# One ACT function for the second layer's activation, and weight absolute values on DVE

## The chip, the core and the metric

The kernel runs on one core of a Trainium2 chip. The core's engines each work through a queue of their own, in order: TensorE (PE in the profile, with its weight loads as PEld), VectorE (DVE), ScalarE (ACT), GpSimd (POOL) and SyncE (SP, which here only issues transfers). Engines wait for one another through semaphores. The metric is the device time of one execution in microseconds (us), as the median of several runs.

## What is computed

The reference does causal attention with a local mask for half of the heads and a strided mask for the other half (4 sequences of 576 positions, 8 heads of 64), then two feed-forward layers on the 2304 tokens of 512 features, each with 2048 hidden features. Everything is float32. The layers differ in their activation:

```
h = x @ w_in                       # first layer
g = h * clip(h + 3, 0, 6) / 6      # "hard swish"
x = g @ w_out

h = x @ w_in                       # second layer
sp = log1p(exp(h))                 # h itself above 20
g = h * tanh(sp)                   # "Mish"
out = g @ w_out
```

## The kernel before

**Precision.** Each float32 product is made of three matmuls: every operand is split into a high part and a low part (`xh` and `xl` for the layer's input, `gh` and `gl` for the activation's result, `w(0)` and `w(1)` for a weight), and `mm3` adds low weight times high value, high weight times low value and high times high into one PSUM bank (L804, L805, L806).

**Steps.** The tokens are cut into blocks of 512, 512, 512, 256 and 512 columns, and the 16 chunks of 128 hidden features of a layer into groups (4, 6, 6 in the first layer, 6, 5, 5 in the second). One step is one block with one chunk: 80 steps a layer. A step has twelve matmuls that make `h` in a PSUM bank, the activation, the split of the result, and twelve matmuls that add the chunk's share to four banks of output sums. The first kind reads `xh` and `xl`, the second `gh` and `gl`, so they can be told apart in the trace.

**Between the two kinds of matmul.** In the first layer ACT makes a clipped line of `h` from PSUM into a buffer `t` (L812) and DVE multiplies it by `h` (L815). In the second layer `mish` (L820 to L853) does eight passes: Tanh from PSUM (L836), Square (L837), Exp (L839) on ACT, a line that may go to ACT, DVE or POOL (L832, L834), then a DVE product (L843), Square on ACT (L845), a DVE product (L848) and a DVE product with `h` (L852), after which the bank of `h` is free. In both layers the high part is then copied, by ACT in this kernel (`gh`, L337), and the low part subtracted on POOL (`gl`, L900).

**Weights.** They come as 64-bit numbers, in 64 pieces (the input half and the output half of 16 chunks in 2 layers, numbered k from 0 to 63), by one DMA each. `decode` (L738 to L798) takes each apart: absolute value (L759 on ACT or L761 on DVE), then DVE passes (L766, L770, L775), a copy of the high part on ACT (L337), and further DVE passes up to the low part (L781, L785, L789, L793). There are 16 slots for ready weights. A slot is free when the last block of its group has used it.

**Order.** Nothing is ordered by the compiler. `Plan` holds each operation with a cost, the operations it depends on, a bank or two and a due time, and `run` makes a list schedule of it ahead of time: it takes the operation that can start first by these costs, and among those near to each other the one due first. Due times of matmuls follow the steps, those of the activation follow from them backwards. Where an operation may run on several engines, `run` chooses. The instructions are then written out in that order, and every engine keeps to it. A change of a cost or of the number of operations can so move any instruction behind it.

Of the kernel before, what the change touches and what calls it, by code (L numbers as in the profile page):

```python
# [7 lines left out]
F32 = mybir.dt.float32  # L8
# [3 lines left out]
AF = mybir.ActivationFunctionType  # L12
ALU = mybir.AluOpType
PSUM = bass.MemoryType.PSUM

P = 128
# [24 lines left out]
EARLY_SUMS = 2  # L41

N_RAW, N_WA, N_WM, N_T, N_G = 3, 3, 2, 4, 4
N_SEED = 2
N_QKV, N_E, N_PT = 2, 4, 2

BANKS = {
    "first": (0, 1, 2, 3, 4, 5, 6, 7),
# [37 lines left out]

LEAD = 0.8883

SEED = (0.67959831, 1.31360091, 0.35009874)
STEP = (0.1250005420051549, -1.500006504050999, 0.7499978319855396)  # L90


class Op:
# [26 lines left out]
class Plan:  # L120
# [9 lines left out]
    def add(self, engine, cost, emit, deps=(), due=None, bank=None, frees=None, lock=""):  # L130
        costs = cost if isinstance(cost, dict) else {engine: cost}
        op = Op(costs, emit, deps, due, bank, frees, lock)
        self.ops.append(op)
        return op
# [140 lines left out]
def act_ns(n, psum=False):  # L275
    return (50 if psum else 95) + 0.84 * n


def dve_ns(n):
    return 70 + 1.05 * n  # L280
# [6 lines left out]
def copy_ns(n, psum=False):  # L287

    return {"act": act_ns(n, psum), "dve": dve_ns(n if psum else n / 2)}
# [4 lines left out]
    return {"dve": dve_ns(n), "pool": pool_ns(n)}  # L294


def line_ns(n):

    return {"act": act_ns(n), "dve": dve_ns(n / 2), "pool": 50 + 1.05 * n}


def mm3_ns(n):

    return 3 * (n + 32) / 2.4
# [7 lines left out]
def attention_then_two_ffns(ctx, tc, qkv, masks, wts, out):  # L312
# [3 lines left out]
    nc = tc.nc  # L316
    B, NPAIR = qkv.shape[:2]
    DM, NT = out.shape
# [7 lines left out]
    N = max(BLOCKS)  # L326
# [5 lines left out]
    add = plan.add  # L332
    engines = {"dve": nc.vector, "pool": nc.gpsimd}
# [8 lines left out]
    pool = ctx.enter_context(tc.tile_pool(name="main", bufs=1, side="right"))  # L342
# [8 lines left out]
    gh_t = [pool.tile([P, N], F32R, name=f"gh{k}") for k in range(N_G)]  # L351
    gl_t = [pool.tile([P, N], F32R, name=f"gl{k}") for k in range(N_G)]

    offset = pool.tile([P, 1], F32, name="offset")
    raw_t = [pool.tile([P, DM], U64, name=f"raw{k}") for k in range(N_RAW)]
    wa_t = [pool.tile([P, DM], F32, name=f"wa{k}") for k in range(N_WA)]
    wm_t = [pool.tile([P, DM], F32, name=f"wm{k}") for k in range(N_WM)]
# [24 lines left out]
    pt_t = [ap_.tile([P, (HS + 2) * P], F32, name=f"pt{k}") for k in range(N_PT)]  # L382
    zeros = words[:, n_v:][:, :FILL]
    scratch = ap_.tile([P, 1], F32, name="scratch")
    late = []

    def open_late():

        att.__exit__(None, None, None)
        lp = ctx.enter_context(tc.tile_pool(name="late", bufs=1, side="left"))  # L390
        w_t.extend(lp.tile([P, 2, DM], F32R, name=f"w{k}") for k in range(2 * EARLY_SLOTS, 2 * SLOTS))
        ys.extend(lp.tile([P, KC, BLOCKS[j]], F32, name=f"y{j}") for j in range(EARLY_SUMS, len(BLOCKS)))
        late.extend(lp.tile([P, N], F32, name=f"seed{k}") for k in range(N_SEED))


    class Record:
# [3 lines left out]
    for m in range(2):  # L400
        for g, n in enumerate(GROUPS[m]):
            walk = LAST_WALK if (m, g) == (1, len(GROUPS[1]) - 1) else range(len(blocks))
            for j in walk:
                for c in range(n):
                    s = Record()
# [7 lines left out]
    t = START  # L413
# [310 lines left out]
    closing = add("act", 0, open_late, attended)  # L724
# [8 lines left out]
    t = 1e12  # L733
    for k in order[::-1]:
        t = w_due[k] = min(w_due[k] - EARLY_W, t - HALF_PACE)
    w_ready, w_ops = {}, []

    def decode(k):  # L738


        m, c, half = order[k]
        raw, a, rest = raw_t[k % N_RAW], wa_t[k % N_WA], wm_t[k % N_WM]
        words = raw.bitcast(U32).rearrange("p (n t) -> p n t", t=2)
        low, high = words[:, :, 0], words[:, :, 1]
        ai, resti = a.bitcast(U32), rest.bitcast(U32)
        slot = k % (2 * SLOTS)
        w = lambda part: w_t[slot][:, part]
        old = w_ops[k - N_RAW]["raw"] if k >= N_RAW else []
        old_a = w_ops[k - N_WA]["end"] if k >= N_WA else None
        old_m = w_ops[k - N_WM]["end"] if k >= N_WM else None  # L750
        if k >= 2 * SLOTS:
            old_w = w_use[order[k - 2 * SLOTS]]
        else:
            old_w = [closing] if slot >= 2 * EARLY_SLOTS else []
        load = add("dma", dma_ns(8 * P * DM), lambda: nc.sync.dma_start(raw, wts[m, c, half]), old)

        def magnitude(eng):
            if eng == "act":
                nc.scalar.activation(a, high.bitcast(F32), AF.Abs)  # L759
            else:  # L760
                nc.vector.tensor_scalar(ai, high, 0x7FFFFFFF, None, ALU.bitwise_and)  # L761

        o = add(None, copy_ns(DM), magnitude, [load, old_a], lock=("dve",))
        o = add(
            "dve", dve_ns(DM / 2),
            lambda: nc.vector.tensor_scalar(a, a, TINY, HUGE, ALU.max, ALU.min), [o], lock=("dve",),  # L766
        )
        o = add(
            "dve", dve_ns(DM / 2),
            lambda: nc.vector.tensor_scalar(ai, ai, 3, 0x3FFFF000, ALU.logical_shift_left, ALU.bitwise_and),  # L770
            [o], lock=("dve",),
        )
        hi = add(
            "dve", dve_ns(DM),
            lambda: nc.vector.scalar_tensor_tensor(ai, high, 0xC0000000, ai, ALU.bitwise_and, ALU.bitwise_or),  # L775
            [o], lock=("dve",),
        )
        o = add(None, copy_ns(DM), lambda eng: copy(eng, w(0), a), [hi, *old_w], lock=("dve",))
        power = add(
            "dve", dve_ns(DM / 2),  # L780
            lambda: nc.vector.tensor_scalar(ai, ai, 0xFF800000, None, ALU.bitwise_and), [o], lock=("dve",),  # L781
        )
        o = add(
            "dve", dve_ns(DM / 2),
            lambda: nc.vector.tensor_scalar(resti, high, 0x1FF, None, ALU.bitwise_and), [load, old_m], lock=("dve",),  # L785
        )
        o = add(
            "dve", dve_ns(DM),
            lambda: nc.vector.scalar_tensor_tensor(rest, resti, 2.0 ** 32, low, ALU.mult, ALU.add), [o], lock=("dve",),  # L789
        )  # L790
        lo = add(
            "dve", dve_ns(DM),
            lambda: nc.vector.scalar_tensor_tensor(w(1), rest, 2.0 ** -52, a, ALU.mult, ALU.mult),  # L793
            [o, power, *old_w], lock=("dve",),
        )
        lo.due = w_due[order[k]]
        w_ops.append({"raw": [hi, o], "end": lo})
        w_ready[order[k]] = lo  # L798
# [16 lines left out]
            lambda: nc.vector.scalar_tensor_tensor(t, t, 1.0, h(), ALU.min, ALU.mult), [o], frees=s.h,  # L815
        )

    mish_ends = {}

    def mish(s, prod, free):  # L820


        n = s.n
        t = t_t[s.id % N_T][:, :n]
        h = lambda: banks[s.h.n][:, :n]
        seed = lambda: late[s.id % N_SEED][:, :n]
        a, b, c = SEED
        scale, bias, more = STEP

        def line(eng):  # L830
            if eng == "act":
                nc.scalar.activation(seed(), seed(), AF.Copy, bias=a, scale=b)  # L832
            else:
                engines[eng].tensor_scalar(seed(), seed(), b, a, ALU.mult, ALU.add)  # L834

        o = add("act", act_ns(n, True), lambda: nc.scalar.activation(t, h(), AF.Tanh, scale=0.5), [prod, free])  # L836
        o = add("act", act_ns(n), lambda: nc.scalar.activation(t, t, AF.Square, bias=1.0, scale=-1.0), [o])  # L837
        w = o
        o = add("act", act_ns(n), lambda: nc.scalar.activation(seed(), t, AF.Exp, scale=-c), [o, mish_ends.get(s.id - N_SEED), closing])  # L839
        o = add(None, line_ns(n), line, [o], lock=("dve", "pool"))  # L840
        o = add(
            "dve", dve_ns(n),
            lambda: nc.vector.scalar_tensor_tensor(t, t, 4.0, seed(), ALU.add, ALU.mult), [o], lock=("dve",),  # L843
        )
        o = add("act", act_ns(n), lambda: nc.scalar.activation(t, t, AF.Square, bias=offset, scale=scale), [o])  # L845
        o = mish_ends[s.id] = add(
            "dve", dve_ns(n),
            lambda: nc.vector.scalar_tensor_tensor(t, t, more, seed(), ALU.add, ALU.mult), [o], lock=("dve",),  # L848
        )
        return add(  # L850
            "dve", dve_ns(n),
            lambda: nc.vector.scalar_tensor_tensor(t, t, 1.0, h(), ALU.subtract, ALU.mult), [o], frees=s.h,  # L852
        )  # L853

    x_parts = {}
    opened, closed = None, []
# [4 lines left out]
    for s in steps:  # L861
        n, k_in, k_out = s.n, (s.m, s.c, 0), (s.m, s.c, 1)
# [8 lines left out]
        prod = opened  # L871
        for kc in range(KC):
# [10 lines left out]
            prod = add("pe", cost, emit, [prod, w_ready[k_in], *deps, *before], due=s.at + (kc + 1) * cost, bank=s.h if kc == 0 else None)  # L883
# [9 lines left out]
        o = (hard_swish, mish)[s.m](s, prod, old.low if old else pairs[3].values[0])  # L893
        t = t_t[s.id % N_T][:, :n]
# [13 lines left out]
        for d in range(KC):  # L908
# [21 lines left out]
            due = op.due + 3000  # L930
            before = y_sums.get((s.j, d)) or ([closing] if s.j >= EARLY_SUMS else attended[:2 * NPAIR])
            if s.grp == 0:
                o = add(None, copy_ns(n, True), lambda eng, y=y, src=src: copy(eng, y(), src()), [op, *before], due=due, frees=bank)
                y_sums[s.j, d] = [o]
                continue
            o = add(
                "dve", dve_ns(n),
                lambda y=y, src=src: nc.vector.tensor_tensor(y(), src(), y(), ALU.add), [op, *before], due=due, frees=bank,  # L938
            )
# [17 lines left out]
        if s.closes:  # L957
            w_use[k_out].extend(s.out)

    add("dve", 60, lambda: nc.vector.memset(offset, STEP[1]), due=1000)  # L960


    cleared = add("dve", 520, lambda: nc.vector.memset(zeros, 0.0), due=0)
    add("act", 1300, lambda: nc.scalar.activation(scratch, zeros[:, :1], AF.Exp), [cleared], due=2500)
    plan.filler = cleared, 3 + 4 * FILL / 2.4, lambda n: nc.tensor.matmul(  # L965
# [75 lines left out]
```

## Time and profile before

| what | us |
| --- | --- |
| median of 3 runs | 883.15 |
| lowest and highest run | 882.71, 885.07 |
| profiled execution, first to last instruction (span) | 880.7 |
| PE busy, DVE busy, ACT busy, POOL busy | 859.2, 581.2, 506.8, 275.0 |
| last matmul ends | 877.0 |

The profile is of one execution and gives its span. A time of the profiled execution by the other clock is not given; the runs' median lies 2.45 us above the span. Matmuls are pipelined, and each row of one has a modelled end, so that the rows of neighbours overlap. The pace of PE is read from one start to the next.

### The profile page before, as it was taken

To read this page: it belongs to the slowest core of one execution; us is meant where nothing else is said; L and a number is where in the kernel's file an instruction comes from. 1 tells how busy PE (TensorE), PEld (TensorE's weight loads), DVE (VectorE), ACT (ScalarE), POOL (GpSimd) and SP (SyncE) were. 2 spreads that over 40 slices of the span, in tenths; PEclk is the share of its full clock that TensorE was granted. 3 is DMA by queue.
4 is the path that set the end of the run, shared out by engine and by line. 5 is a ranking of instruction groups with operands and counts; after the bars stand their busy time and mean duration, and the time that the engine had idled before them with its cause. 6 is when DMAs were issued, how large, how long until landed. Compare 5 with 4: busy or idle time off the path is not lost.

```text
span 880.7 us, 15660 instructions
## 1 busy us (share of the span) xinstructions
PE 859.2 (98%) x6326; PEld 715.5 (81%) x6326; DVE 581.2 (66%) x985; ACT 506.8 (58%) x943; POOL 275.0 (31%) x245
## 2 busy tenths in 40 slices
PE   5899999999999999999999999999999999999998
PEld 2567888888888988888888888898888888888887
DVE  5688778899221599812269887457887867655554
ACT  2566765653222244423346787778887777666664
POOL 4544552322222222344351522221222222222222
PEclk9899999999999999999999999999999999999999
DMA  8846543233000023300003112000221100010112
GB/s 255 235 149 182 183 134 98 72 96 117 3 1 1 25 73 96 96 1 1 1 25 99 45 52 69 1 1 25 72 73 49 48 1 1 0 48 1 48 48 72
DMA packets 19499, 57.16 MB, mean 65 GB/s; under 512 B 2916, under 2 KB 5604, under 8 KB 19428
## 3 DMA queue, kind: packets, MB, share of 16 engines
q1 hardware_dynamic: 18768, 56.01, 20.9%
q8 instruction: 49, 0.80, 0.4%
q10 hardware_dynamic: 660, 0.16, 0.1%
q14 instruction: 22, 0.18, 0.1%
HBM read 51.45 MB, written 4.72 MB: 64 GB/s over the span
## 4 chain that ended last, share of the span: by engine, by line
PE 94%; DMA 2%; DVE 1%; issue 1%; ACT 1%; ACTq 0%; POOL 0%; SPq 0%; DVEq 0%
PE bank L804 30%; PE bank L805 30%; PE bank L806 29%; PE bank L681 2%; PE bank L575 2%; DMA qk<-in_qkv_dram 1%; PE bank L965 1%; DMA v<-in_qkv_dram 1%; PE bank L642 1%; DMA mk_odd<-in_masks_dram 1%; ACT pt L337 0%; PE bank L644 0%; DVE sum L623 0%; DVE wa L775 0%; ACTq L481 0%
## 5 line engine op out<-in xcount | busy, mean ns | idle before, releaser
L900 POOL TENSOR_TENSOR gl<-t,gh 128x512 fp32r<-128x512 f32 (+1 forms) x160 | 198.1, 1239 | 532.1 <-ACT gh L337 486.1
L804 PE MATMUL bank<-xh,w 128*128 128x512 f32 (+1 forms) x640 | 237.4, 371 | 0.6 <-DVE w L793 0.6
L804 PE MATMUL bank<-gh,w 128*128 128x512 f32 (+1 forms) x640 | 237.9, 372 | 0.0
L805 PE MATMUL bank<-xl,w 128*128 128x512 f32 (+1 forms) x640 | 236.4, 369 | 0.0
L805 PE MATMUL bank<-gl,w 128*128 128x512 f32 (+1 forms) x640 | 236.2, 369 | 0.0
L806 PE MATMUL bank<-xh,w 128*128 128x512 f32 (+1 forms) x640 | 235.4, 368 | 0.0
L806 PE MATMUL bank<-gh,w 128*128 128x512 f32 (+1 forms) x640 | 235.4, 368 | 0.0
L815 DVE SCALAR_TENSOR_TENSOR t<-t,bank 128x512 f32<-128x512 f32 (+1 forms) x80 | 50.6, 633 | 136.5 <-ACT t L812 136.2
L804 PEld LDWEIGHTS bank<-xh,w 128*128 128x128 f32 x640 | 120.6, 188 | 22.0 <-DVE w L793 0.8
L804 PEld LDWEIGHTS bank<-gh,w 128*128 128x128 f32 x640 | 120.4, 188 | 20.9
L806 PEld LDWEIGHTS bank<-xh,w 128*128 128x128 f32 x640 | 120.5, 188 | 20.7
L806 PEld LDWEIGHTS bank<-gh,w 128*128 128x128 f32 x640 | 120.3, 188 | 20.6
L805 PEld LDWEIGHTS bank<-xl,w 128*128 128x128 f32 x640 | 120.7, 189 | 19.7
L805 PEld LDWEIGHTS bank<-gl,w 128*128 128x128 f32 x640 | 120.5, 188 | 19.0
L812 ACT ACTIVATE t<-bank 128x512 f32<-128x512 f32 (+1 forms) x80 | 44.4, 556 | 143.5 <-PE bank L806 143.2
L337 ACT CAST gh<-t 128x512 fp32r<-128x512 f32 (+1 forms) x160 | 91.7, 574 | 51.8 <-DVE t L815 32.1
L843 DVE SCALAR_TENSOR_TENSOR t<-t,seed 128x512 f32<-128x512 f32 (+1 forms) x80 | 77.4, 967 | 59.4 <-ACT seed L832 57.5
L848 DVE SCALAR_TENSOR_TENSOR t<-t,seed 128x512 f32<-128x512 f32 (+1 forms) x80 | 58.0, 726 | 45.0 <-ACT t L845 44.9
L845 ACT ACTIVATE t<-t,offset 128x512 f32<-128x512 f32 (+1 forms) x80 | 54.4, 680 | 51.2 <-DVE t L843 51.2
L836 ACT ACTIVATE t<-bank 128x512 f32<-128x512 f32 (+1 forms) x80 | 44.3, 553 | 27.2 <-PE bank L806 26.4
L789 DVE SCALAR_TENSOR_TENSOR wm<-wm,raw 128x512 f32<-128x512 uint32 x64 | 57.5, 899 | 0.2
L938 DVE TENSOR_TENSOR y<-bank,y 128x512 f32<-128x512 f32 (+1 forms) x80 | 48.5, 633 | 11.6 <-PE bank L806 11.1
(61 smaller groups left out, 842.0 us busy)
## 6 DMA issues: line engine op xcount, KB each, us to landing
raw<-in_wts_dram SPq DMA_DIRECT2D x64, 512.0 KB, 3.6
qk<-in_qkv_dram SPq DMA_DIRECT2D x14, 576.0 KB, 5.3
v<-in_qkv_dram SPq DMA_DIRECT2D x14, 432.0 KB, 5.3
out_dram<-y SPq DMA_DIRECT2D x16, 256.0 KB, 2.0
y<-in_qkv_dram SPq DMA_DIRECT2D x2, 576.0 KB, 8.8
out_dram<-y SPq DMA_DIRECT2D x4, 128.0 KB
v<-in_qkv_dram SPq DMA_DIRECT2D x14, 32.0 KB, 5.2
y<-in_qkv_dram SPq DMA_DIRECT2D x1, 432.0 KB
```

The costliest lines, as they stand in the source:

```text
L337: nc.scalar.copy(out, src)
L789: lambda: nc.vector.scalar_tensor_tensor(rest, resti, 2.0 ** 32, low, ALU.mult, ALU.add), [o], lock=("dve",),
L804: nc.tensor.matmul(o, a[:, 1], high, start=first, stop=False)
L805: nc.tensor.matmul(o, a[:, 0], low, start=False, stop=False)
L806: nc.tensor.matmul(o, a[:, 0], high, start=False, stop=last)
L812: o = add("act", act_ns(n, True), lambda: nc.scalar.activation(t, h(), AF.Relu, bias=0.5, scale=1.0 / 6.0), [prod, free])
L815: lambda: nc.vector.scalar_tensor_tensor(t, t, 1.0, h(), ALU.min, ALU.mult), [o], frees=s.h,
L843: lambda: nc.vector.scalar_tensor_tensor(t, t, 4.0, seed(), ALU.add, ALU.mult), [o], lock=("dve",),
L845: o = add("act", act_ns(n), lambda: nc.scalar.activation(t, t, AF.Square, bias=offset, scale=scale), [o])
L848: lambda: nc.vector.scalar_tensor_tensor(t, t, more, seed(), ALU.add, ALU.mult), [o], lock=("dve",),
L900: lambda eng, gh=gh, gl=gl, t=t: engines[eng].tensor_tensor(gl, t, gh.bitcast(F32), ALU.subtract),
L938: lambda y=y, src=src: nc.vector.tensor_tensor(y(), src(), y(), ALU.add), [op, *before], due=due, frees=bank,
```

## The change

The eight passes of `mish` become one ACT instruction with the function Mish, from the PSUM bank into `t`; it frees the bank itself. The buffers `seed` and `offset` and the planner's cost `line_ns` go. In `decode` the absolute value of pieces k = 20 to 63 is set on DVE; before, the planner chose (ACT for 63 of the 64). Nothing else is edited; the planner is run on the new list of operations. Lines of `mish` after are L813 to L818, those of the absolute value L749 to L758.

```diff
+ABS_ON_ACT = 20
...
-        o = add(None, copy_ns(DM), magnitude, [load, old_a], lock=("dve",))
+        if k < ABS_ON_ACT:
+            o = add(None, copy_ns(DM), magnitude, [load, old_a], lock=("dve",))
+        else:
+            o = add("dve", dve_ns(DM / 2), lambda: magnitude("dve"), [load, old_a], lock=("dve",))
...
     def mish(s, prod, free):
...
-        o = add("act", act_ns(n, True), lambda: nc.scalar.activation(t, h(), AF.Tanh, scale=0.5), [prod, free])
-        o = add("act", act_ns(n), lambda: nc.scalar.activation(t, t, AF.Square, bias=1.0, scale=-1.0), [o])
...
-        return add(
-            "dve", dve_ns(n),
-            lambda: nc.vector.scalar_tensor_tensor(t, t, 1.0, h(), ALU.subtract, ALU.mult), [o], frees=s.h,
-        )
+        return add("act", act_ns(n, True), lambda: nc.scalar.activation(t, h(), AF.Mish), [prod, free], frees=s.h)
...
-    add("dve", 60, lambda: nc.vector.memset(offset, STEP[1]), due=1000)
```

On ACT, at the switch from the first layer to the second. Before (L812 is the first layer's pass, L836 the first of a second layer's step, L337 a copy, `t` the activation's buffer, `gh` the high part):

```order
L812 ACTIVATE t_106<-bank1_62 128x512
L337 CAST w10_79<-wa0_101 128x512
L836 ACTIVATE t_106<-bank0_61 128x512
L337 CAST gh3_92<-t_106 128x512
L837 ACTIVATE t_106<-t_106 128x512
L759 ACTIVATE wa2_103<-raw2_100 128x512
L839 ACTIVATE seed0_2314<-t_106 128x512
L832 ACTIVATE seed0_2314<-seed0_2314 128x512
L845 ACTIVATE t_106<-t_106,offset_97 128x512
```

The same place after:

```order
L807 ACTIVATE t_105<-bank3_64 128x512
L332 CAST gh3_92<-t_105 128x512
L818 ACT_TABLE_LOAD
L818 ACTIVATE t_105<-bank1_62 128x512
L332 CAST gh0_89<-t_105 128x512
L332 CAST w10_79<-wa0_100 128x512
L818 ACTIVATE t_105<-bank2_63 128x512
L332 CAST w11_80<-wa1_101 128x512
L332 CAST gh1_90<-t_105 128x512
```

A second load of an activation table stands in front of the first Mish pass, the only one besides that at the kernel's start. The copy of the high part follows its pass directly, and Square, Exp, line, Square and the absolute value are gone from between.

On PE, in the second layer, where step 140's result is used for the first time. Before (`gh0` is the high part of step 140, `w6` the slot of the weight that made its `h`, so that `xh` with `w12` makes the `h` of the third step after it):

```order
L804 MATMUL bank0_61<-xh2_83,w12_2307 128x512
L805 MATMUL bank0_61<-xl2_87,w12_2307 128x512
L806 MATMUL bank0_61<-xh2_83,w12_2307 128x512
L804 MATMUL bank0_61<-xh3_84,w12_2307 128x512
L805 MATMUL bank0_61<-xl3_88,w12_2307 128x512
L806 MATMUL bank0_61<-xh3_84,w12_2307 128x512
L804 MATMUL bank3_64<-gh0_89,w7_76 128x512
```

After:

```order
L799 MATMUL bank0_61<-xh2_83,w10_79 128x512
L800 MATMUL bank0_61<-xl2_87,w10_79 128x512
L801 MATMUL bank0_61<-xh2_83,w10_79 128x512
L799 MATMUL bank0_61<-xh3_84,w10_79 128x512
L800 MATMUL bank0_61<-xl3_88,w10_79 128x512
L801 MATMUL bank0_61<-xh3_84,w10_79 128x512
L799 MATMUL bank7_68<-gh0_89,w7_76 128x512
```

The use of a step's result follows the `h` of the second step after it (slot `w10`) instead of the third (slot `w12`). Counted in the order, 72 matmuls stood between the end of a step's `h` and the first use of its result, and 48 stand there now, as in the first layer of either kernel.

On DVE, at the first piece of weights that the edit moves, k = 20 (in `wa2`, from `raw2`). Before:

```order
L781 TENSOR_SCALAR wa1_102<-wa1_102 128x512
L766 TENSOR_SCALAR wa2_103<-wa2_103 128x512
L793 SCALAR_TENSOR_TENSOR w3_72<-wm1_105,wa1_102 128x512
L815 SCALAR_TENSOR_TENSOR t_106<-t_106,bank0_61 128x512
L770 TENSOR_SCALAR wa2_103<-wa2_103 128x512
L785 TENSOR_SCALAR wm0_104<-raw2_100 128x512
L775 SCALAR_TENSOR_TENSOR wa2_103<-raw2_100,wa2_103 128x512
```

After:

```order
L776 TENSOR_SCALAR wa1_101<-wa1_101 128x512
L753 TENSOR_SCALAR wa2_102<-raw2_99 128x512
L788 SCALAR_TENSOR_TENSOR w3_72<-wm1_104,wa1_101 128x512
L810 SCALAR_TENSOR_TENSOR t_105<-t_105,bank0_61 128x512
L761 TENSOR_SCALAR wa2_102<-wa2_102 128x512
L780 TENSOR_SCALAR wm0_103<-raw2_99 128x512
L765 TENSOR_SCALAR wa2_102<-wa2_102 128x512
L770 SCALAR_TENSOR_TENSOR wa2_102<-raw2_99,wa2_102 128x512
```

One more pass stands at the head of the piece (L753), and the passes behind it move back by one place. The queues of SP are the same in both, and on PE, ACT and DVE everything ahead of piece 20 stands in the same order, but for the one small memset of `offset` on DVE.

## Rows read from the trace of the kernel before

**Rows 1.** The page's head: span, and busy time of each engine.
```profile
span 880.7 us, 15660 instructions
PE 859.2 (98%) x6326; PEld 715.5 (81%) x6326; DVE 581.2 (66%) x985; ACT 506.8 (58%) x943; POOL 275.0 (31%) x245
```
**Rows 2.** Windows: stretch, length, busy us and instructions by engine, clock, DMA share, GB/s.
```profile
0.00:76.00 76.00, 58.19 (x1327) 40.05 (x1327) 54.73 (x125) 35.51 (x79) 35.47 (x50) 0.96 0.73 213
...
180.00:476.00 296.00, 296.00 (x1440) 250.05 (x1439) 163.46 (x263) 106.86 (x188) 94.34 (x76) 1.00 0.14 43
476.00:877.00 401.00, 401.00 (x1946) 338.59 (x1944) 279.48 (x435) 299.31 (x546) 103.67 (x86) 1.00 0.12 36
```
**Rows 3.** Waits: waiting instruction, releaser, us in total, times, longest.
```profile
PE bank L804 <- DVE w L793: 0.6, 1, 0.6
```
**Rows 4.** Windows: a calm stretch of layer one, a crowded one of layer two.
```profile
200.00:300.00 100.00, 100.00 (x496) 84.84 (x495) 36.59 (x59) 26.11 (x48) 24.89 (x21) 1.00 0.08 25
600.00:700.00 100.00, 100.00 (x452) 82.97 (x451) 81.64 (x137) 80.89 (x142) 25.03 (x19) 1.00 0.18 56
```
**Rows 5.** Timeline of PE in those stretches: start us, us, instruction.
```profile
220.48 0.39 PE L806 MATMUL bank<-xh,w 128*128 128x512 f32 x1
...
231.64 0.39 PE L804 MATMUL bank<-gh,w 128*128 128x512 f32 x1
...
673.23 0.39 PE L806 MATMUL bank<-xh,w 128*128 128x512 f32 x1
...
689.85 0.39 PE L804 MATMUL bank<-gh,w 128*128 128x512 f32 x1
```
**Rows 6.** The chain that ended last, its end: start us, us, what.
```profile
876.00 1.49 DVE y L938 x4
```
**Rows 7.** Groups of instructions: busy us, mean ns | idle before them, releasers.
```profile
L836 ACT ACTIVATE t<-bank 128x512 f32<-128x512 f32 (+1 forms) x80 | 44.3, 553 | 27.2 <-PE bank L806 26.4 <-POOL gl L900 0.3
L843 DVE SCALAR_TENSOR_TENSOR t<-t,seed 128x512 f32<-128x512 f32 (+1 forms) x80 | 77.4, 967 | 59.4 <-ACT seed L832 57.5 <-POOL seed L834 1.6
L848 DVE SCALAR_TENSOR_TENSOR t<-t,seed 128x512 f32<-128x512 f32 (+1 forms) x80 | 58.0, 726 | 45.0 <-ACT t L845 44.9
L852 DVE SCALAR_TENSOR_TENSOR t<-t,bank 128x512 f32<-128x512 f32 (+1 forms) x80 | 50.3, 629 | 1.5
```
**Rows 8.** Timelines of PE, ACT, DVE, POOL: step 140 from `h` to use.
```profile
774.99 0.39 PE L806 MATMUL bank<-xh,w 128*128 128x512 f32 x1
...
775.48 0.60 ACT L836 ACTIVATE t<-bank 128x512 f32<-128x512 f32 x1 [0.28 <-PE bank L806]
...
781.40 0.69 DVE L852 SCALAR_TENSOR_TENSOR t<-t,bank 128x512 f32<-128x512 f32 x1
...
782.75 0.60 ACT L337 CAST gh<-t 128x512 fp32r<-128x512 f32 x1
...
783.49 1.30 POOL L900 TENSOR_TENSOR gl<-t,gh 128x512 fp32r<-128x512 f32 x1 [4.15 <-ACT gh L337]
...
791.62 0.39 PE L804 MATMUL bank<-gh,w 128*128 128x512 f32 x1
```
**Rows 9.** Timeline of ACT at the start: the one table load, and what follows.
```profile
7.25 1.28 ACT L964 ACT_TABLE_LOAD   x1 [7.25 <-DMA mk_str<-in_masks_dram]
8.55 0.20 ACT L964 ACTIVATE scratch<-t 128x1 f32<-128x1 f32 x1
```
**Rows 10.** Groups: the absolute value on ACT and on DVE.
```profile
L759 ACT ACTIVATE wa<-raw 128x512 f32<-128x512 f32 x63 | 42.3, 673 | 17.1 <-DMA raw<-in_wts_dram 11.4 <-DVE w L793 2.8 <-DVE wa L770 1.9
...
L761 DVE TENSOR_SCALAR wa<-raw 128x512 uint32<-128x512 uint32 x1 | 0.4, 428 | 3.1 <-DMA raw<-in_wts_dram 3.1
```
**Rows 11.** Timelines of DVE and PE: weight piece 52 ready, and first used.
```profile
627.40 0.69 DVE L793 SCALAR_TENSOR_TENSOR w<-wm,wa 128x512 fp32r<-128x512 f32 x1
...
642.74 0.39 PE L804 MATMUL bank<-xh,w 128*128 128x512 f32 x1
```
**Rows 12.** Window of layer two, line L337 alone: length, ACT busy, clock, DMA.
```profile
476.00:877.00 401.00, 71.19 (x127) 1.00 0.12 36
```

More of the change, by code (lines that the diff above doesn't have):

```diff
@@ L43 @@
 N_RAW, N_WA, N_WM, N_T, N_G = 3, 3, 2, 4, 4
-N_SEED = 2
 N_QKV, N_E, N_PT = 2, 4, 2
+ABS_ON_ACT = 20
 BANKS = {
@@ L87 @@
 LEAD = 0.8883
-SEED = (0.67959831, 1.31360091, 0.35009874)
-STEP = (0.1250005420051549, -1.500006504050999, 0.7499978319855396)
 class Op:
@@ L294, in plain_ns @@
     return {"dve": dve_ns(n), "pool": pool_ns(n)}
-def line_ns(n):
-    return {"act": act_ns(n), "dve": dve_ns(n / 2), "pool": 50 + 1.05 * n}
 def mm3_ns(n):
@@ L352, in attention_then_two_ffns @@
     gl_t = [pool.tile([P, N], F32R, name=f"gl{k}") for k in range(N_G)]
-    offset = pool.tile([P, 1], F32, name="offset")
     raw_t = [pool.tile([P, DM], U64, name=f"raw{k}") for k in range(N_RAW)]
@@ L384, in attention_then_two_ffns @@
     scratch = ap_.tile([P, 1], F32, name="scratch")
-    late = []
     def open_late():
@@ L392, in open_late @@
         ys.extend(lp.tile([P, KC, BLOCKS[j]], F32, name=f"y{j}") for j in range(EARLY_SUMS, len(BLOCKS)))
-        late.extend(lp.tile([P, N], F32, name=f"seed{k}") for k in range(N_SEED))
     class Record:
@@ L816, in hard_swish @@
         )
-    mish_ends = {}
     def mish(s, prod, free):
@@ L825, in mish @@
         h = lambda: banks[s.h.n][:, :n]
[L826 to L834, printed above, removed]
-        o = add("act", act_ns(n, True), lambda: nc.scalar.activation(t, h(), AF.Tanh, scale=0.5), [prod, free])
-        o = add("act", act_ns(n), lambda: nc.scalar.activation(t, t, AF.Square, bias=1.0, scale=-1.0), [o])
[L838 to L841, printed above, removed]
-            "dve", dve_ns(n),
-            lambda: nc.vector.scalar_tensor_tensor(t, t, 4.0, seed(), ALU.add, ALU.mult), [o], lock=("dve",),
-        )
[L845 to L849, printed above, removed]
-        return add(
-            "dve", dve_ns(n),
-            lambda: nc.vector.scalar_tensor_tensor(t, t, 1.0, h(), ALU.subtract, ALU.mult), [o], frees=s.h,
-        )
+        return add("act", act_ns(n, True), lambda: nc.scalar.activation(t, h(), AF.Mish), [prod, free], frees=s.h)
     x_parts = {}
```

## The prediction

> **What bounds the kernel now.** I read the page's head first. PE is busy for 859.2 of 880.7 us, DVE for 581.2 and ACT for 506.8 [rows 1]. That alone does not say that PE sets the time, since a busy share is a mean over stages, so I read the windows next. In the first 76 us PE is busy for 58.2 us; in these 76 us attention starts up, and this is where PE is idle. From 180 to 476 us it is busy for 296.00 of 296.00 us, and from 476 to 877 us for 401.00 of 401.00, at a clock of 1.00 [rows 2]. The second layer's activation lies in the last of these windows and the moved absolute values in the last two, so every instruction that the change takes away or moves stands where PE has no idle time that the profile shows.
>
> A busy PE could still be a slow one, because the rows of matmuls overlap. So I read its pace, from start to start. In a calm stretch of the first layer (200 to 300 us, DVE busy 36.6%, ACT 26.1%) and in a crowded one of the second (600 to 700 us, 81.6% and 80.9%) [rows 4] I take the last matmul of one step's `h` and the first that reads that step's result. By the order these are 49 matmuls apart in the first layer and 73 in the second. 231.64 - 220.48 = 11.16 us over 49 is 227.8 ns; 689.85 - 673.23 = 16.62 us over 73 is 227.7 ns [rows 5]. PE goes at one pace, whatever DVE and ACT do. The list of waits agrees: PE waited for a ready weight once, for 0.6 us [rows 3], during attention, and for a step's activation never.
>
> At the end, the last of four DVE sums begins to run out at 876.00 + 1.49 = 877.49 us [rows 6], and the last output transfer follows, to 880.7. Nothing of the activation is left by then.
>
> **The change part by part.**
>
> *The eight passes.* What does the path get back? Before, step 140 takes this way: its last `h` matmul starts at 774.99, Tanh at 775.48, the last of the eight passes ends at 781.40 + 0.69 = 782.09, the high part is copied at 782.75 and the low part is done at 783.49 + 1.30 = 784.79. The first matmul that needs it starts at 791.62 [rows 8]. The result lies ready for 6.8 us before PE takes it. Of these eight passes, nothing is on the path that sets the end. Removing them is worth 0 us as long as PE stays busy, however much DVE gets back (77.4 + 58.0 + 50.3 = 185.7 us from its three products [rows 7]).
>
> *The new pass.* No row shows Mish. The nearest is Tanh, also one function from the same bank into the same buffer: 553 ns in the mean of both widths [rows 7], 0.60 us at 512 columns [rows 8]. From above, it can hardly take longer than the whole chain it replaces, 782.09 - 775.48 = 6.61 us at 512 columns. I take 0.60 us, because the operands are the same. The price to the path is 0 at this value, and I keep the upper end for a rival. The range has no end below nothing from here: a shorter pass gives PE nothing that it waits for.
>
> *The new order on PE.* The planner puts a step's second matmuls 48 instead of 72 matmuls behind its `h`. The cover shrinks from 72 x 0.2277 = 16.4 us to 48 x 0.2277 = 10.9 us. Is it still enough? From Tanh's start to the end of the low part the shortened way is 0.60 + 0.02 to the copy, 0.60 for the copy, 0.14 to POOL (783.49 - 782.75 - 0.60) and 1.30 there: 2.7 us, where the 0.02 is the gap between two instructions of ACT that follow one another [rows 9]. From the end of the last `h` matmul, one pace after its start (775.22), to Tanh it is 0.3 us [rows 8]. That makes 3.0 us of 10.9 and leaves 7.9 us, more than the 6.8 us of before. In the last step of all, with 256 columns, the order leaves 48 short matmuls, about half as long; the way is shorter there too. Cost: 0 us. The same matmuls are done, so a changed order does not change their sum.
>
> *The table load.* The order shows one more, in front of the first Mish pass. The only one in the trace took 1.28 us, and the next ACT instruction started 0.02 us after its end [rows 9]. Behind it on ACT wait the Mish of the layer's first step, its copy, and the copy of a weight piece; POOL's subtraction and then PE wait for these. The first step's cover of 7.9 us falls to 6.6 us. Cost: 0 us.
>
> The Trainium skill (ScalarE: Activation LUTs, section What ACT_TABLE_LOAD costs) adds a drain of about 1380 ns to every switch, 2.66 us in all. By it the cover would fall to 5.2 us, an estimate from that page, and the sum would still be 0. The row here shows 1.28 us alone; nothing had run on ACT before it, so that it cannot show what a drain costs.
>
> *Absolute values on DVE.* 44 passes of 673 ns leave ACT and 44 of 428 ns come to DVE [rows 10], 18.8 us in all. In the first layer this lengthens the longest unbroken run of pieces, k = 24 to 35, by 12 x 0.43 = 5.1 us at most, and DVE is idle for 296.0 - 163.5 = 132.5 us of that stretch [rows 2]. In the second layer the removed products pay for it many times over. The least time between a ready piece and its first use, from k = 20 on, is that of k = 52: ready at 628.09, used at 642.74, 14.7 us [rows 11]. Were its cover gone, a piece would cost 0.43 us; with 14.7 us of it, 0 us.
>
> *Head and tail.* Up to the first edited piece, at 180 us, the orders on PE and ACT are the same, and that on DVE lacks one memset of `offset` that is no part of the attention's way. The tail has the same four sums and transfers. Both 0 us.
>
> The sum is 0 against the profiled span of 880.7 us. The runs' median lies 2.45 us above that span, and I take the same distance: 883.15, so **883.1 us**.
>
> **The rivals.**
>
> *PE gets faster because DVE and ACT leave it alone.* If they had slowed the matmuls, the pace would differ between the two stretches. It differs by 0.1 ns, with a reading error of about 0.02 us over 49 or 73 matmuls, 0.4 ns [rows 5]. At 0.4 ns the 1920 matmuls of the second layer would give 0.8 us: 882.3. To reach 0.3% (2.65 us), about what a measurement of this kernel can tell from no change, it would take 1.4 ns each. Without that, a gain of this size needs a cause that I do not see, such as a luckier attention start out of the 17.8 us that PE is idle there [rows 2]; 3 us of it would give 880.
>
> *A new wait of PE, at the switch of layers or at a block's end.* For it speaks that the cover is a third shorter and the table load is new. Against it speaks 3.0 us of need under 10.9 us of cover. If the table load came wholly through, it would cost 1.28 us; if some five steps lost 1 us each from late copies behind it, 5 us: 888. It decides once a result needs more than 10.9 us, which is longer than even the eight-pass way from 774.99 to 784.79 took.
>
> *Mish is slow, the rival that ends slower.* One ACT instruction per step can become the bound, since in the second layer everything on ACT must fit beside PE. The copies there take 71.2 us [rows 12]; with the table load, (401.0 - 71.2 - 1.3) / 80 = 4.1 us is left for each Mish, in the mean. From there on ACT, not PE, sets the layer's time. At the upper end, 6.61 us at 512 columns, about 6.1 in the mean (scaled as Tanh's 553 to 600), ACT needs 80 x 6.1 + 72.5 = 560 us, 159 above 401: 1042 us. Against it speaks Tanh's 553 ns [rows 7]: Mish would have to take more than seven times as long with the same operands.
>
> The Trainium skill (the same page, section Step-by-step: what each stage is for) holds that the time per element is the same for every function, and lists 19 tried. By it this rival falls away; no run here shows Mish yet.
>
> **How the numbers follow.** I give no change 0.90. The gain on PE or at the start gets 0.05, the new wait 0.03, slow Mish 0.02. The first case itself spans what the runs shown span, 882.71 to 885.07, and the 0.8 us of a faster pace below it. I take 881.4 to 885.3 as the range, the runs' own spread with a little over 1 us below, which leaves out the rivals' larger prices and the ends of the first case, together not more than 2 in 10. Faster by over 0.3%: 0.05; within: 0.90; slower: 0.03 + 0.02 = 0.05.
>
> **What would show it.** Right: PE again busy without a gap from 76 us to about 877, the last sums again near 876; two table loads of 1.28 us; 80 Mish passes near 553 ns in the mean; 45 absolute values on DVE near 430 ns and 19 on ACT; DVE's busy time near 581 - 186 + 19 = 414 us. Between a step's `h` and its use the low part should lie ready for about 8 us. Wrong: a wait of PE for `gl`, `gh` or `w` behind 180 us; a Mish pass above 4 us; a pace in the second layer more than 1 ns from 227.7. A time that differs while all these hold would lie in the first 76 us, and would have nothing to do with the activation.

## The result, and the profile after

The changed kernel takes 888.93 us in the median against 882.93 for the one before: the ratio is 1.0073, with a 95% interval of 1.0052 to 1.0095. It is about 6 us slower. No change was forecast.

The head of the page after, and two of its windows (stretch, length, busy us and instructions of PE, PEld, DVE, ACT, POOL, clock, DMA share, GB/s), to be held against [rows 1, 2]:

```profile
span 888.8 us, 15050 instructions
PE 866.9 (98%) x6326; PEld 716.5 (81%) x6326; DVE 441.9 (50%) x788; ACT 309.3 (35%) x581; POOL 276.8 (31%) x244
```

```profile
180.00:476.00 296.00, 296.00 (x1425) 247.53 (x1424) 170.37 (x278) 91.04 (x162) 93.80 (x76) 1.00 0.13 40
476.00:877.00 401.00, 401.00 (x1898) 334.32 (x1898) 133.35 (x223) 116.80 (x208) 104.63 (x84) 1.00 0.11 37
```

DVE got back 139 us and ACT 197 us, and PE is still busy without a gap, at a clock of 1.00. But within the same 296 us PE started 1425 matmuls instead of 1440, and within the same 401 us 1898 instead of 1946. It is slower while it is busy, and it is so in the first layer too, whose activation was not touched.

The list of waits of PE after (instruction, releaser, us, times, longest) has seven rows; its largest and its last two are these. All of them end in the first 76 us, and none is for `gh`, `gl` or `w`:

```profile
PE bank L567 <- DMA qk<-in_qkv_dram: 6.1, 2, 4.4
...
PE bank L634 <- ACT pt L332: 0.8, 2, 0.4
PE bank L634 <- POOL e L625: 0.8, 1, 0.8
```

So I read the pace. The timeline of PE after (start us, us, instruction), first at the same step 27 of the first layer as in [rows 5], then the last matmul:

```profile
221.69 0.39 PE L801 MATMUL bank<-xh,w 128*128 128x512 f32 x1
...
233.08 0.39 PE L799 MATMUL bank<-gh,w 128*128 128x512 f32 x1
...
884.81 0.28 PE L801 MATMUL bank<-gh,w 128*128 128x256 f32 x1
```

The 49 matmuls take 11.39 us, 232.4 ns each, against 227.8 before. The last matmul before is this one:

```profile
876.74 0.28 PE L806 MATMUL bank<-gh,w 128*128 128x256 f32 x1
```

From step 27's last `h` matmul to the last matmul of all it is 884.81 - 221.69 = 663.12 us, and 876.74 - 220.48 = 656.26 before. These 6.86 us are the loss in the two traces (6.0 us between the medians of the runs). The two profiled spans differ by 8.1 us; the other 1.2 us lie ahead of step 27, which these two executions reached at different times (221.69 against 220.48). That is no more than repeated runs of one kernel differ by: those of the kernel before span 880.88 to 885.07 us. I use this stretch below, "step 27 to the end", as the measure for a trace.

Not all of PE is slow. Two places of the second layer after, in the timeline of PE. First weights from the slots w12 to w15 (here `gh` with w13), then only w0 to w11:

```profile
642.60 0.39 PE L799 MATMUL bank<-gh,w 128*128 128x512 f32 x1
642.83 0.40 PE L800 MATMUL bank<-gl,w 128*128 128x512 f32 x1
643.07 0.39 PE L801 MATMUL bank<-gh,w 128*128 128x512 f32 x1
643.30 0.39 PE L799 MATMUL bank<-gh,w 128*128 128x512 f32 x1
643.53 0.40 PE L800 MATMUL bank<-gl,w 128*128 128x512 f32 x1
643.77 0.39 PE L801 MATMUL bank<-gh,w 128*128 128x512 f32 x1
644.00 0.40 PE L799 MATMUL bank<-xh,w 128*128 128x512 f32 x1
```

```profile
520.15 0.39 PE L799 MATMUL bank<-xh,w 128*128 128x512 f32 x1
...
521.51 0.39 PE L799 MATMUL bank<-gh,w 128*128 128x512 f32 x1
```

The first six take 1.40 us, 233 ns each. The six from 520.15 to 521.51 take 1.36 us, 227 ns each. The slots tell them apart. The order of the build says which slot each matmul of the trace reads. From 180 us on, matmuls of 512 columns start 232.9 ns apart in the mean at slots w12 to w15 after, and 229.1 before. At w0 to w11 it is 229.1 after and 227.1 before, and the slow ones after are neighbours of w12 to w15: up to six matmuls away from one of those the mean is 231.1 ns (226.8 before), farther away 227.3 in both.

What is special about these slots is where they lie. In SBUF, the memory that holds all these buffers, w0 to w11, xh, xl, gh, gl, `offset`, and then the raw weights and `t` lie in one pool that is laid out against a fixed upper end; w12 to w15 lie in another pool at the lower end. The change took out `offset`, 4 bytes in a place of 32. By the addresses of the build everything in front of it moved up by 32 bytes: w0 from 42944 to 42976, xh0 from 92096 to 92128, and the others alike. The raw weights and `t` stayed, and w12 stayed at 1152. All 16 slots, their parts and columns, and all pieces of xh, xl, gh and gl have one remainder modulo 256 in their pool. So one number describes each layout: the distance of w12 to w15 from the data (xh, xl, gh, gl), which is the address of the weight less that of the data, modulo 256. It was 1152 - 92096 = -90944, which is 192 modulo 256, and after the change 1152 - 92128 gives 160.

### The profile page after: what moved, and what is told of

Its sections match the earlier page's. It is cut to its first block, busy times and chain, and to the rows that moved or that the text cites. A ratio compares the mean times of both kernels' runs of the same rounds, so it can differ in the third digit from the quotient of the medians.

```text
span 888.8 us, 15050 instructions
## 1 busy us (share of the span) xinstructions
PE 866.9 (98%) x6326; PEld 716.5 (81%) x6326; DVE 441.9 (50%) x788; ACT 309.3 (35%) x581; POOL 276.8 (31%) x244
## 4 chain that ended last, share of the span: by engine, by line
PE 95%; DMA 2%; issue 1%; ACT 1%; DVE 0%; POOL 0%; ACTq 0%; SPq 0%
PE bank L799 30%; PE bank L800 30%; PE bank L801 29%; PE bank L673 2%; PE bank L567 2%; DMA qk<-in_qkv_dram 1%; PE bank L927 1%; PE bank L634 1%; DMA v<-in_qkv_dram 1%; DMA mk_str<-in_masks_dram 1%; PE bank L636 0%; ACT pt L332 0%; DVE y L903 0%; DVE wa L770 0%; POOL e L625 0%
## 5 line engine op out<-in xcount | busy, mean ns | idle before, releaser
L865 POOL TENSOR_TENSOR gl<-t,gh 128x512 fp32r<-128x512 f32 (+1 forms) x160 | 201.1, 1257 | 544.1 <-ACT gh L332 455.3
L818 ACT ACTIVATE t<-bank 128x512 f32<-128x512 f32 (+1 forms) x80 | 44.5, 556 | 244.5 <-PE bank L801 244.4
L776 DVE TENSOR_SCALAR wa<-wa 128x512 uint32<-128x512 uint32 x64 | 40.9, 640 | 107.7 <-ACT w L332 107.1
L332 ACT CAST w<-wa 128x512 fp32r<-128x512 f32 x64 | 39.6, 620 | 47.9 <-DVE wa L770 24.3
L770 DVE SCALAR_TENSOR_TENSOR wa<-raw,wa 128x512 uint32<-128x512 uint32 x64 | 54.6, 854 | 0.5
L784 DVE SCALAR_TENSOR_TENSOR wm<-wm,raw 128x512 f32<-128x512 uint32 x64 | 49.5, 774 | 0.1
```

What stands on the lines that cost most here:

```text
L332: nc.scalar.copy(out, src)
L818: return add("act", act_ns(n, True), lambda: nc.scalar.activation(t, h(), AF.Mish), [prod, free], frees=s.h)
L865: lambda eng, gh=gh, gl=gl, t=t: engines[eng].tensor_tensor(gl, t, gh.bitcast(F32), ALU.subtract),
```

## The experiments

Theory P (place): the distance sets the pace of PE, and the removed buffer changed it. Rival W (work): something that the change does on ACT, DVE or in PE's order slows the matmuls. None of these kernels leaves out a part of the computation.

**The buffer back, in the changed kernel** (`a_main32`):

```diff
     gl_t = [pool.tile([P, N], F32R, name=f"gl{k}") for k in range(N_G)]
+    pool.tile([P, 8], F32, name="pad")
```

> The changed kernel with an unused buffer of 32 bytes per partition where `offset` lay; nothing is computed otherwise. Theory P (place): the removed `offset` moved w0 to w11, xh, xl, gh and gl up by 32 bytes against w12 to w15, and by that slowed the matmuls. Then this kernel is back at the time of the one before, 883 us, with matmul pace 227 ns for slots w0 to w11 and 229 for w12 to w15. Theory W (work: the Mish pass, the table load, the absolute values on DVE or the new order slow PE): it stays at 889 us, since all of these are still in.

It takes 881.94 us, a ratio of 0.9994 (0.9986 to 1.0003). Its PE timeline, step 27 and the last matmul:

```profile
219.81 0.39 PE L802 MATMUL bank<-xh,w 128*128 128x512 f32 x1
...
875.85 0.28 PE L802 MATMUL bank<-gh,w 128*128 128x256 f32 x1
```

656.04 us, where the kernel before has 656.26. This kernel has the same instructions in the same order as the changed one, with all the new work and the table load, and the loss is gone. W is out.

**The same shift in the kernel before** (`b_main32`, the same line in the old kernel, which shifts by 32 bytes the other way):

> The kernel before with 32 bytes more in the same pool: w0 to w11, xh, xl, gh and gl move down by 32 bytes, everything else stays, with the same instructions in the same order. Theory P: about 889 us (6 us slower), pace of matmuls around slots w12 to w15 at 232 to 236 ns. Theory W: 883 us, as before.

886.70 us, ratio 1.0059 (1.0042 to 1.0077), with not one instruction changed: about 5 us slower, where the expectation had 6. Its PE timeline:

```profile
219.47 0.39 PE L807 MATMUL bank<-xh,w 128*128 128x512 f32 x1
...
880.18 0.28 PE L807 MATMUL bank<-gh,w 128*128 128x256 f32 x1
```

660.71 us, 4.5 more than before. The distance is 224 here, another than after.

**The changed kernel's own distance in the kernel before** (`b_late480`):

```diff
         lp = ctx.enter_context(tc.tile_pool(name="late", bufs=1, side="left"))
+        lp.tile([P, 120], F32, name="pad")
```

> The kernel before, instructions and order untouched, with 480 bytes in front of w12: w12 to w15 then lie to the data (xh, xl, gh, gl) as in the changed kernel, 160 bytes apart modulo 512, where they lie 192 apart in the kernel before. Theory P: about 888 us, 6 slower, and a pace near 233 ns at slots w12 to w15. If a part of the change's own work adds to the slowdown (old order and old activation protect PE): less, 884 to 886 us.

889.76 us, ratio 1.0083 (1.0069 to 1.0097). Its PE timeline:

```profile
219.60 0.39 PE L807 MATMUL bank<-xh,w 128*128 128x512 f32 x1
...
882.57 0.28 PE L807 MATMUL bank<-gh,w 128*128 128x256 f32 x1
```

662.97 us, within 0.15 us of the changed kernel's 663.12. The old order and the old activation protect PE from nothing. The distance of 160 gives the whole loss by itself.

**Distance, or the operands' own address?** (`a_late32`: the pad of the late pool in the changed kernel, 32 bytes.)

> The changed kernel with 32 bytes in front of w12 in the late pool, so that w12 to w15 (and the late sums) move up as the others did. Theory P1 (the distance between w12 to w15 and the other operands counts): 883 us. Theory P2 (operands must themselves lie on a multiple of 64 bytes): 889 us or more, since now none does. Theory W: 889 us.

882.44 us, ratio 1.0005 (0.9991 to 1.0019), step 27 to the end 656.04 us. No weight and no data operand lies on a multiple of 64 bytes here, and the pace is that of the kernel before. P1 holds and P2 falls.

**Weights to data, or weights to weights?** (`a_wx32`: 32 bytes between w11 and xh0 in the changed kernel.)

```diff
     w_t = [pool.tile([P, 2, DM], F32R, name=f"w{k}") for k in range(2 * EARLY_SLOTS)]
+    pool.tile([P, 8], F32, name="pad")
```

> The changed kernel with 32 bytes between w11 and xh0: w0 to w11 move down by 32 bytes, the data stay, so that all 16 slots lie at another place modulo 64 than the data. Theory PD (a weight's distance to the data streamed beside it counts): all matmuls slow to 231 to 234 ns, so 3840 matmuls lose some 4 to 6 ns each at 512 columns, 12 to 20 us: 894 to 902 us. Theory PW (the distance between weights in different slots counts): w0 to w11 and w12 to w15 again lie as in the kernel before, so 882 us.

897.17 us, ratio 1.0167 (1.0150 to 1.0183), as PD has it. Its PE timeline:

```profile
222.10 0.40 PE L802 MATMUL bank<-xh,w 128*128 128x512 f32 x1
...
891.35 0.27 PE L802 MATMUL bank<-gh,w 128*128 128x256 f32 x1
```

669.25 us, 13 more than before. Slots w0 to w11 now run at 233.2 ns too. What counts is a weight's place against the data; between the weights of different slots the distance is that of the kernel before.

**Which distances.** Four more pads of the late pool in the changed kernel, of 352, 96, 416 and 480 bytes, and one of 320 in the kernel before:

> The changed kernel with 352 bytes in front of w12, so that w12 to w15 lie at the same address modulo 512 as w0 to w11, xh, xl, gh and gl. Theory P1, if equal places are best: faster than before, since w12 to w15 then run at 227 instead of 229 ns; about 750 matmuls of 512 columns times 2.3 ns is 1.7 us, so 881 us. Theory P2 and W: 889 us.

> The changed kernel with 96 bytes in front of w12: w12 to w15 lie 256 bytes from the data modulo 512. If only the place modulo 64 counts: pace at w12 to w15 as in the kernel before, 229 ns, 882.4 us. If the place modulo 256 counts: 227 ns, 881 us.

> The changed kernel with 416 bytes in front of w12: w12 to w15 lie 64 bytes from the data modulo 512. If only multiples of 64 count: 227 or 229 ns at w12 to w15, 881 to 882.4 us. If a small distance is bad however it divides: 232 ns or more, 886 us or more.

> The changed kernel with 480 bytes in front of w12: w12 to w15 lie 128 bytes from the data modulo 256, the one multiple of 64 not yet tried. If every multiple of 64 but 64 itself is cheap: 227 to 229 ns at these slots, 881 to 882.5 us. If only equal places modulo 256 are free and 192 is the exception: 232 ns or more, 886 us or more.

> The kernel before with 320 bytes in front of w12, so that w12 to w15 lie at the data's place modulo 512. Theory P: pace 227 ns at all slots, about 1 us faster than before, 881 us. If the gain seen at equal places needed the new activation: 882 us and 229 ns at w12 to w15.

All traces in one table. The paces are mean distances between starts, of matmuls of 512 columns from 180 us on; the last column is the ratio of times to those of the kernel before on the same chip.

| kernel | distance, w12 to w15 | ns at w12 to w15 | ns at w0 to w11 | step 27 to end, us | ratio (95%) |
| --- | --- | --- | --- | --- | --- |
| before | 192 | 229.1 | 227.1 | 656.26 | 1 |
| changed | 160 | 232.9 | 229.1 | 663.12 | 1.0073 (1.0052 to 1.0095) |
| a_main32 | 192 | 229.1 | 227.0 | 656.04 | 0.9994 (0.9986 to 1.0003) |
| a_late32 | 192 | 229.1 | 227.0 | 656.04 | 1.0005 (0.9991 to 1.0019) |
| b_late480 | 160 | 233.1 | 229.0 | 662.97 | 1.0083 (1.0069 to 1.0097) |
| b_main32 | 224 | 233.1 | 228.0 | 660.71 | 1.0059 (1.0042 to 1.0077) |
| a_late416 | 64 | 233.3 | 228.7 | 662.01 | 1.0065 (1.0045 to 1.0084) |
| a_late480 | 128 | 233.2 | 228.9 | 663.01 | 1.0078 (1.0053 to 1.0103) |
| a_late352 | 0 | 227.2 | 227.1 | 655.46 | 0.9991 (0.9980 to 1.0001) |
| a_late96 | 0 | 227.2 | 227.2 | 655.46 | 0.9988 (0.9973 to 1.0004) |
| b_late320 | 0 | 227.1 | 227.2 | 655.56 | 0.9991 (0.9980 to 1.0002) |
| a_wx32 | 160; 224 at w0 to w11 | 232.4 | 233.2 | 669.25 | 1.0167 (1.0150 to 1.0183) |

At distance 0 all slots run at one pace, and 256 (`a_late96`, counted modulo 512) is as good as 0 (`a_late352`), so that here the place modulo 256 counts; for the other distances no second value modulo 512 was tried. At 192 the slots cost 2 ns, at the other four tried 6 ns. Multiples of 64 are not enough: 64 and 128 are slow. Nor is it the size of the gap: 64 and 192 lie equally far from 0 on its two sides, and cost 6 and 2 ns. The guess in the expectation of `a_late416`, that a small distance is bad, does not explain it either: 128 is as bad.

The three kernels at distance 0 are the best by the trace, 0.7 to 0.8 us less than before and alike to 0.1 us. By time each is 0.1% below the kernel before, and each interval still reaches 1. They beat the changed kernel clearly, and no gain over the kernel before is shown.

**The two halves of the change**, at the old distance of 192. First the absolute values on DVE alone, with the eight passes kept (`d_only`, the condition `k < 20` in the old kernel's `decode`):

> The kernel before with only the second part: absolute values from k = 20 on DVE, the eight passes kept, addresses as before. By the prediction's sum 0: 882 us. If DVE, which is the busiest beside PE in the second layer's weight bursts, now makes PE wait for w: more than 884 us, with a wait of PE for DVE in the list.

882.88 us, ratio 1.0002 (0.9991 to 1.0014). Its PE timeline:

```profile
223.14 0.39 PE L809 MATMUL bank<-xh,w 128*128 128x512 f32 x1
...
879.40 0.28 PE L809 MATMUL bank<-gh,w 128*128 128x256 f32 x1
```

656.26 us, the same to the last digit as before. Then Mish alone (`m_only`, the changed kernel with `ABS_ON_ACT = 64` and the 32 bytes of `a_main32`):

> The changed kernel without its second part: the planner may put any absolute value on ACT again (63 of 64 go there), and 32 unused bytes keep the addresses of the kernel before. The order then has 34 table loads, since the absolute value and Mish stand in different sets by it. If a table load is hidden as the prediction says (cover 7.9 us, 1.28 us each, two around an absolute value): 882 us, and PE never waits in the second layer. If the loads or a drain come through: each pair costs up to 2.6 us, 16 pairs up to 41 us.

883.43 us, ratio 1.0005 (0.9993 to 1.0016). Its table loads, by line (busy us, mean ns | idle before, releasers), and one of the sequences on ACT:

```profile
L819 ACT ACT_TABLE_LOAD x17 | 21.8, 1283 | 6.1 <-PE bank L802 5.9
L752 ACT ACT_TABLE_LOAD x16 | 20.5, 1283 | 3.4 <-DMA raw<-in_wts_dram 3.1
```

```profile
482.41 0.62 ACT L332 CAST w<-wa 128x512 fp32r<-128x512 f32 x1
483.05 1.28 ACT L752 ACT_TABLE_LOAD   x1
484.34 0.68 ACT L752 ACTIVATE wa<-raw 128x512 f32<-128x512 f32 x1
485.42 1.28 ACT L819 ACT_TABLE_LOAD   x1 [0.40 <-PE bank L802]
486.72 0.60 ACT L819 ACTIVATE t<-bank 128x512 f32<-128x512 f32 x1
```

33 loads in the second layer, 42 us of ACT, and PE has one wait there, of 0.4 us, where the expectation had none. It is for ACT's copy of an output sum, which stood behind the load at 637.54 us:

```profile
PE bank L800 <- ACT y L332: 0.4, 1, 0.4
```

So the second part of the change avoids 32 table loads. In the traces this is worth 0.8 us (656.87 us from step 27 to the end against 656.04 in `a_main32`, one trace each); in the times of the runs it is not shown, since the two intervals overlap.

## Why the prediction was wrong

**What held.** Each step on ACT, DVE and PE's order came out as worked out. Mish and the absolute value (busy us, mean ns | idle before):

```profile
L818 ACT ACTIVATE t<-bank 128x512 f32<-128x512 f32 (+1 forms) x80 | 44.5, 556 | 244.5 <-PE bank L801 244.4
L753 DVE TENSOR_SCALAR wa<-raw 128x512 uint32<-128x512 uint32 x45 | 20.4, 453 | 3.2 <-DMA raw<-in_wts_dram 3.2
```

Mish takes 556 ns in the mean, as Tanh did (553 [rows 7]), so the rival of a slow Mish is out. The Trainium skill (ScalarE: Activation LUTs, section Step-by-step: what each stage is for) holds that the time per element is the same for every function; these two means bear it out for Mish. Step 140 goes this way after, to be held against [rows 8]:

```profile
784.13 0.40 PE L801 MATMUL bank<-xh,w 128*128 128x512 f32 x1
784.63 0.60 ACT L818 ACTIVATE t<-bank 128x512 f32<-128x512 f32 x1 [4.20 <-PE bank L801]
785.26 0.62 ACT L332 CAST gh<-t 128x512 fp32r<-128x512 f32 x1
786.01 1.29 POOL L865 TENSOR_TENSOR gl<-t,gh 128x512 fp32r<-128x512 f32 x1 [4.15 <-ACT gh L332]
795.54 0.40 PE L799 MATMUL bank<-gh,w 128*128 128x512 f32 x1
```

From Mish to the end of the low part it is 787.30 - 784.63 = 2.67 us, forecast 2.7. The result then lies ready for 8.2 us, forecast 7.9. The second table load took its 1.28 us and made PE wait for nothing. In `m_only` a load starts 0.02 us after the end of the copy ahead of it (482.41 + 0.62 = 483.03), and the next instruction 0.01 us after the load. The Trainium skill (ScalarE: Activation LUTs, section What ACT_TABLE_LOAD costs) adds a drain of about 1380 ns to every switch; these rows show none. The sum of the work is 0, as forecast: `a_main32` is at 0.9994 of the time before. DVE's busy time fell less than forecast, to 441.9 instead of 414 us, mostly since some of its other passes got longer (the clamp of a weight piece, L766 before and L761 after, from 449 to 594 ns); it is 442.3 in `a_main32` as well, where the time is that of before, so this has no part in the result.

**What failed.** The step that failed is "The same matmuls are done, so a changed order does not change their sum", with "PE goes at one pace, whatever DVE and ACT do" under it. The sum priced every matmul as in the trace of before, and had no term for what the removed `offset` does to the addresses of the buffers that stay. The term is 2 ns in the mean on each matmul at w0 to w11 and 4 at w12 to w15, 6.9 us from step 27 to the end. The one rival that spoke of a changed pace looked for its cause in the work of other engines, and had it faster; the sign and the cause were both wrong. The list of signs did name "a pace in the second layer more than 1 ns from 227.7", and this sign came: matmuls of 512 columns start 230.0 ns apart there in the mean, 227.7 before. But the pace moved in the first layer as well (230.5 against 227.7), where no rival had a cause for it.

**Could it have been seen?** The means of 49 and 73 matmuls that I read [rows 5] hid a small form of it, since about half of each read w12 to w15: 229.1 ns at w12 to w15 in the kernel before, 227.1 elsewhere, 2 ns that no other engine's work explained. Split by slot, these would have shown that the place of an operand has a price. That the price at another distance is three times as high could not be read there.

**What stays open.** How the chip comes to it was not tested. The runs show that the distance modulo 256 between a weight and the streamed data decides, not by which access. The slow pace also spreads from w12 to w15 to their neighbours at w0 to w11, and why it does is open. So is the difference of 2.4 us between the distances 224 and 160. The pace at w12 to w15 is the same for both; at w0 to w11 it is 228.0 ns for 224 and 229.1 for 160, and some 1,900 matmuls there make 2.1 us of it.

## What to carry to other kernels

Where PE is busy without a gap, removing or adding a buffer can be an edit of the matmuls, since the buffers around it move: compare the addresses of weights and streamed operands before and after, and keep their distance modulo 256 with a pad of a few bytes. This is shown for the matmuls of this kernel alone (128x128 weights in fp32r, mostly 512 columns). When a kernel with less work gets slower without a wait, count the starts of matmuls in equal windows and split their pace by operand slot before looking at the engines that changed. Then put back the old layout alone, which separates what the change does from where it left things.

## What the runs showed that was not expected

An unused buffer of 32 bytes per partition takes 7 us off the changed kernel in one place (a ratio of 0.9994 against 1.0073) and adds 8 us to it in another (1.0167). It adds about 5 us to the kernel before (1.0059). All operands lie on multiples of 32 bytes throughout. Traces of one layout agree closely from step 27 to the end: 656.26 us for both the kernel before and `d_only`, which differ in the work of DVE and ACT, 656.04 for both `a_main32` and `a_late32`, and 655.46 for both `a_late352` and `a_late96`. Step 27 itself is reached between 219.27 and 223.14 us: in these traces most of what differs at one layout lies ahead of it, in the stretch that holds attention.
